# Retention and a bilinear feed-forward layer in one kernel: slots 8 to 11 as one tile, pairs of blocks by 7 products in both four-slot tiles, and a third order of the steps

## The chip, the cores and the metric

The kernel runs on one core of a Trainium2 chip. The time is microseconds of the device for one execution of the whole program, median of the runs; lower is better. The kernel before takes 218.17 us (median of 3 runs, 218.07 to 218.31).

The engines are named as in the profile: PE (TensorE, matrix products; PEld is its weight load), DVE (VectorE), ACT (ScalarE), POOL (GpSimd) and SP (SyncE, which only issues transfers here). Each engine works through its own list of instructions in the order in which the program emits them; engines wait for each other by semaphores.

## The reference

The input is q, k and v of shape 4 × 8 × 768 × 64 (batch, head, position, width) and the weights w_a, w_b (512 × 1536) and w_out (1536 × 512), all float32.

```python
    state = np.zeros((B, H, D, D), dtype=np.float32)
    y = np.zeros_like(q)
    for t in range(S):
        state = gamma[None, :, None, None] * state + np.einsum('bhd,bhe->bhde', k[:, :, t], v[:, :, t])
        y[:, :, t] = scale * np.einsum('bhd,bhde->bhe', q[:, :, t], state)
...
    x = np.ascontiguousarray(attn_out.transpose(0, 2, 1, 3)).reshape(B * S, H * D)
...
    a = x @ w_a
    b = x @ w_b
    return (a * b @ w_out).astype(np.float32)
```

The loop runs over the 768 positions, with gamma_h = 1 − 2^(−5−h) for head h and scale 1/8. The rest is one bilinear feed-forward layer over 3072 tokens.

## The kernel before, in words

**Slots and tiles.** The 3072 tokens are 24 slots of 128: slot t is chunk t mod 6 of batch t div 6. `TILES` (L16) groups the slots for the feed-forward layer: tiles of 4, 2, 2, 2, 2, 4 and 8 slots, so slots 8 and 9 are one tile, 10 and 11 the next, 12 to 15 the four-slot tile numbered 5, and 16 to 23 the last.

**Attention of one slot.** k and q are multiplied by tables of powers of gamma (`scaled`, L318: `kqb<-kf`, `kqb<-qf`, casts to bf16 on the way), v is cast (`vb`). SP turns k and q of a slot around with a transposing DMA (`flip`, L373, L376: `kqT<-kqb`). PE then makes the scores of keys and queries (`scores`, L407: `at<-kqT`; DVE masks them, `aT<-at,mask`, L421), adds k^T v to the state (`update`, L424: `st<-vb,kqb`; a cast to bf16, `gst<-st`), reads the earlier chunks through the state (`inter`, L446: `y<-kqT,gst`), adds the chunk's own part (`intra`, L457: `y<-aT,vb`), and ACT copies the result as columns of x (`leave`, L467: `xt<-y`). Scores of a slot need the turned k and q of both slots of its pair. `turn(new, old)` (L477) makes the scores and states of one pair of slots and the outputs of an earlier pair in one visit.

**The feed-forward layer of a tile.** For each of 12 blocks of 128 columns of the hidden layer, `ffn_a` (L611) and `ffn_g` (L625) make four matmuls each over the tile's tokens (512 columns for four slots, 256 for two). ACT casts the a side (`asb<-a`), and DVE multiplies it with the g side straight from PSUM (`ht<-g,asb`, L633).

**Seven products for eight.** Where two halves times two halves of a matrix product are wanted, the kernel uses a scheme with 7 products and sums ahead of and behind them. The output of each tile from the second on is made this way by class `Group` (products of six 256-column matmuls, `mA`, `mB`, `mC`; sums `hs` of the hidden layer by `hsum`; `wsum` of the weights; results `osb`). In the last tile, all of the hidden layer is made this way by class `Unit` (`uA`, `uB`, `uC`, with weight sums `wea`, `web`, `wsa`, `wsb` from `weight_piece` and `xs` from `x_sum`). In tile 5, `Quad` (L983 on) does so for two of six pairs of blocks (block p and p + 6, p = 0 and 1), a and b separately, each in half banks of 256 columns: ACT copies an intermediate result (`snapf<-fa`, 256 wide), DVE adds and multiplies in 256-wide pieces; `xf` are sums of x.

**What sets the order.** It is written out by hand, in functions that emit one step behind the other: `casts(t)` scales k, q and v of a slot on POOL, turns them on SP and issues the loads of slot t + 2; `blocks(J, a, b)` emits hidden blocks; `single(J, …)` laces a tile's output products with the next tile's first three blocks; `laced` (with the string `LACED`) does it for the tile with pairs; `big` (strings `START` and `END`) is the last tile. Output stores wait in a list until `store()` issues them from SP. PSUM has eight banks: three in a ring for blocks (`Ring`), two for y, two for at, one for st.

Of the kernel before, what the change touches and what calls it, by code (L numbers as in the profile page):

```python
# [9 lines left out]
F32 = mybir.dt.float32  # L10
# [5 lines left out]
TILES = [4, 2, 2, 2, 2, 4, 8]  # L16
# [3 lines left out]
START = ("A1 A2 u0.1 u1.1 A6 T X3 A7 B1 X2 A5 B6 B7 X1 A3 B5 u0.2 u1.2 B2 X4 A4 u0.6 B3 u1.6 B4 u0.5 u1.5 "  # L20
         "u0.7 u2.1 u0.3 u1.7 u2.6 u1.3 u0.4 u2.2 u3.1 u2.5 u1.4 u2.7 u3.6")
END = ("u11.1 u10.5 u10.7 u9.4 u11.6 u10.3 u11.2 S03 a1< u11.5 u11.7 u10.4 b1< u11.3 a1> b1> c1< d1< u11.4 a7 c1> d1> c2 d2 "
       "S02 S01 b7 a2 b2 S04 a6 b6 S13 a5 b5 S12 a3 b3 a4 b4 S11 c7 d7 c6 d6 S14 c5 d5 "
       "c3 c4 d4 d3")
V_LATE = range(12, 20)
LACED = ("X3 X2 m1 m7 m2 a1 b1 a2 b2 m6 X1 a6 b6 a7 b7 F2 X4 m5 a5 b5 K20 G2 a3 b3 a4 b4 V18 "
         "m3 c1 d1 F3 H3 c2 d2 c6 d6 c7 d7 c5 d5 m4 c3 d3 V19 c4 d4 G3")
# [4 lines left out]
def kernel(  # L32
# [78 lines left out]

    def raw_tile(shape, dtype, tag, name):
        return raw.tile(shape, dtype, tag=tag, name=name, bufs=3 if tag == "vf" else 2)
# [3 lines left out]
    def load_slot(t, names="kqv"):  # L117
        b, ci = divmod(t, NCH)
        for nm in names:
            src = {"k": k, "q": q, "v": v}[nm]  # L120
            if nm == "q":
                if t % 2 == 0:
                    load_two(nm, src, b, ci // 2, t)
                continue
            if t % 2 == 0:
                whole[nm] = raw_tile([P, 2, H, D], F32, nm + "f", nm + "f")
            raws[nm, t] = whole[nm][:, t % 2]
            s = src[b, :, ci * P : (ci + 1) * P, :].rearrange("h p d -> p h d")
            seq(nc.sync.dma_start(out=raws[nm, t], in_=s))

    def load_slots(t):
        for u, names in ((t, "kq"), (t + 1, "k"), (t, "v"), (t + 1, "v")):
            load_slot(u, names)

    def load_two(nm, src, b, u, t):
        f = raw_tile([P, H, 2, D], F32, nm + "f", nm + "f")
        s = src[b, :, 2 * u * P : 2 * (u + 1) * P, :].rearrange("h (p two) d -> p h two d", two=2)
        seq(nc.sync.dma_start(out=f, in_=s))  # L138
# [38 lines left out]
    def issue_loads(n):  # L177
        for _ in range(min(n, len(pending))):
# [4 lines left out]
            elif what[0] in "kqv":  # L183
                load_pair_q(n) if what[0] == "q" else load_two(what[0], {"k": k, "v": v}[what[0]], 0, n, 2 * n)
            else:
                {"p": load_pair, "s": load_slots, "t": load_slot, "w": load_w, "o": load_o}[what[0]](n)


    kqb = {}
# [113 lines left out]
    def cast_o(j):  # L303
        cast(nc.gpsimd, wo_bf[:, j * FPO : (j + 1) * FPO, :], wst["o", j])
# [12 lines left out]
    def scaled(eng, t, i):  # L317
        if i and t < 2 * PAIRS:  # L318
# [12 lines left out]
        else:  # L331
            dst = dst.rearrange("p hp r d -> p r hp d")
# [3 lines left out]

    def new_nat(t):
        kqb[t] = nat.tile([P, 2, HP, 2, D], BF16, tag="kqb", name="kqb")
        kb[t], qb[t] = kqb[t][:, 0], kqb[t][:, 1]
        vb[t] = nat.tile([P, H, D], BF16, tag="vb", name="vb")  # L340

    def casts(t, between=lambda: None):
        new_nat(t)
        scaled(nc.gpsimd, t, 0)
        between()
        scaled(nc.gpsimd, t, 1)
        if t not in range(12, 20):
            cast(nc.gpsimd, vb[t], raws["v", t])
        u = t + 2
        if u == 20:  # L350
            load_slot(u, "kq")
        flip(t)
        if u == 20:
            load_slot(u + 1, "k")
            return
        if u == 21:
            load_slot(u - 1, "v")
            load_slot(u, "v")
            load_slot(22, "kq")
            return  # L360
        if u in V_LATE:
            if u == 13:
                load_slot(12, "q")
            elif u == 19:
                load_slot(18, "kq")
            load_slot(u, {12: "k", 18: ""}.get(u, "kq"))
            if u % 2:
                load_slot(u - 1, "v")
                load_slot(u, "v")
        elif u < NSLOT:  # L370
            load_slot(u)

    def flip(t):  # L373
        if t % 2 == 0:
            kqT[t // 2] = tra.tile([P, 2, 2, HP, P], BF16, tag="kqT", name="kqT", bufs=3)
        seq(nc.sync.dma_start_transpose(  # L376
            out=kqT[t // 2][:, t % 2].rearrange("p a b c -> p (a b) c"),
            in_=kqb[t].rearrange("p a hp r d -> p (a hp r d)")))

    def late_kq(t):  # L380
        for u in (t, t + 1):
            new_nat(u)
            scaled(nc.gpsimd, u, 0)
            scaled(nc.gpsimd, u, 1)
            flip(u)
        if t == 20:
            load_slot(23, "k")
            load_slot(22, "v")
            load_slot(23, "v")

    def casts_two(t):
        for u in (t, t + 1):
            new_nat(u)
            scaled(nc.gpsimd, u, 0)
            scaled(nc.gpsimd, u, 1)
            flip(u)
        for u in (t, t + 1):
            cast(nc.gpsimd, vb[u], raws["v", u])
        load_slot(t + 3)
# [9 lines left out]
    def scores(t, where, cuts=2):  # L409
        at = score_banks(where)  # L410
# [13 lines left out]
    def update(t, eng):  # L424
        ci = t % NCH
        if ci == NCH - 1:
            return
# [17 lines left out]

    def inter(t):  # L446
        if t % NCH == 0:
            return
        for j in range(2):
# [8 lines left out]
    def intra(t):  # L458
        for r in range(2):
# [7 lines left out]
    def leave(t):  # L467
        J, i = where[t]
# [7 lines left out]

# [846 lines left out]
```

## Time and profile before

| what | value |
|---|---|
| median of the runs | 218.17 us (218.07 to 218.31, 3 runs) |
| the profiled execution | 218.26 us |
| its span on the core | 216.6 us |
| granted PE clock | 1.0 in every slice |
| busy: PE, DVE, ACT, POOL | 209.8, 151.1, 105.1, 155.5 us |
| instructions of PE, DVE, ACT, POOL | 2250, 277, 236, 187 |

The profile is one execution, taken by the hardware profiler. Its page gives busy time by engine, the span in 40 slices (each digit is tenths of busy time), the chain of work that ended last, and groups of instructions. A group's row reads: line, engine, operation, out<-in, partitions x elements, count | busy us, mean ns of one | idle time of the engine just before them and what ended it. A timeline row reads: start us, duration us (of a run of equal instructions), engine, line, operation, count. In a row of the view of waits stand the engine and what waited, what it waited for, and total us, times, longest. Matmuls overlap in PE's pipeline, so what one costs is read from the distance between starts and not from its duration.

### The profile page before, as it was taken

Reading aid. Unit: us, or ns where it says so; the run is one execution under the profiler, and the core shown is the slowest. Engines: PE = TensorE matmul, PEld = TensorE weight load, DVE = VectorE, ACT = ScalarE, POOL = GpSimd, SP = SyncE. Lnnn points to the kernel's source line nnn. Section 1 sums busy time; section 2 is a strip of 40 time slices with the busy share of each in tenths; the row PEclk is TensorE's granted clock in tenths of the full one; section 3 lists DMA queues with packets and bytes.
Section 4 is the critical chain, followed back from the end, with each engine's and each line's share of the span. In section 5 each row is a group of like instructions: output and inputs, shape, how many; then the busy total and the mean of one; then the engine's idle time right before and its main releaser. Section 6 shows DMA issues by size and latency. Waiting matters only on the chain.

```text
span 216.6 us, 5726 instructions
## 1 busy us (share of the span) xinstructions
PE 209.8 (97%) x2250; PEld 145.8 (67%) x2250; DVE 151.1 (70%) x277; ACT 105.1 (49%) x236; POOL 155.5 (72%) x187
## 2 busy tenths in 40 slices
PE   7789999999999999999999999999999999999994
PEld 3458445587458888888888877557864444458883
DVE  5796347845985486356377978686577887688952
ACT  3175325343224444464576475657545656652331
POOL 7277877778889487979959979799996999530000
PEclk9999999999999999999999999999999999999999
DMA  6999999999999999399989999980013000000055
GB/s 181 315 337 370 377 360 357 363 237 240 227 267 235 173 254 280 76 189 257 213 187 227 222 200 215 236 139 3 5 73 122 0 0 3 2 0 0 27 194 170
DMA packets 82906, 39.68 MB, mean 183 GB/s; under 512 B 57536, under 2 KB 75840, under 8 KB 82880
## 3 DMA queue, kind: packets, MB, share of 16 engines
q1 hardware_dynamic: 82736, 39.26, 74.4%
q8 instruction: 17, 0.28, 0.5%
q10 hardware_dynamic: 144, 0.07, 0.1%
q14 instruction: 9, 0.07, 0.1%
HBM read 28.31 MB, written 6.29 MB: 160 GB/s over the span
## 4 chain that ended last, share of the span: by engine, by line
PE 91%; SPq 3%; DMA 3%; POOL 0%; issue 0%; DVE 0%
PE a L619 18%; PE g L631 18%; PE mA L739 12%; PE uA L913 10%; PE mB L739 6%; PE o L656 5%; PE uB L913 5%; DMA wsta<-in_moe_w_a_dram 3%; PE mC L739 3%; PE at L415 2%; PE uC L913 2%; SPq L150 2%; PE y L463 2%; PE st L433 2%; PE fa L1003 2%; SPq L138 1%
## 5 line engine op out<-in xcount | busy, mean ns | idle before, releaser
L633 DVE TENSOR_TENSOR ht<-g,asb 128x256 bf16<-128x256 f32 (+1 forms) x70 | 34.4, 493 | 30.3 <-PE g L631 27.1
L619 PE MATMUL a<-xt,wa_bf 128*128 128x256 bf16 (+1 forms) x280 | 48.6, 300 | 0.2 <-POOL wa_bf L287 0.2
L631 PE MATMUL g<-xt,wb_bf 128*128 128x256 bf16 (+1 forms) x280 | 48.4, 300 | 0.0
L622 ACT CAST asb<-a 128x256 bf16<-128x256 f32 (+1 forms) x70 | 30.0, 428 | 33.5 <-PE a L619 31.3
L631 PEld LDWEIGHTS <-wb_bf 128*128 128x128 bf16 x280 | 27.1, 98 | 10.2
L619 PEld LDWEIGHTS <-wa_bf 128*128 128x128 bf16 x280 | 26.5, 98 | 10.8 <-POOL wa_bf L287 0.6
L920 ACT COPY snap<-uA 128x512 f32<-128x512 f32 x36 | 20.0, 587 | 15.4 <-PE uA L913 13.9
L335 POOL TENSOR_TENSOR kqb<-kf,ktab 128x512 bf16<-128x512 f32 x22 | 22.9, 1045 | 5.3 <-DMA kf<-in_k_dram 4.9
L739 PEld LDWEIGHTS <-hs 128*128 128x128 bf16 x234 | 22.8, 98 | 3.6
L421 DVE TENSOR_TENSOR aT<-at,mask 128x512 bf16<-128x512 f32 x36 | 22.3, 683 | 0.3
L335 POOL TENSOR_TENSOR kqb<-qf,qtab 128x512 bf16<-128x512 f32 x18 | 19.8, 1100 | 2.6 <-DMA qf<-in_q_dram 1.6
L672 POOL TENSOR_TENSOR ht<-gsb,asb 128x512 bf16<-128x512 bf16 x13 | 15.2, 1174 | 7.5 <-DVE gsb L672 7.4
L746 ACT COPY snaps<-mA 128x256 f32<-128x256 f32 x30 | 11.0, 374 | 18.9 <-PE mA L739 18.9
L672 POOL TENSOR_TENSOR hs<-ht 128x384 bf16<-128x384 bf16 (+3 forms) x14 | 15.8, 1130 | 5.7 <-DMA kf<-in_k_dram 3.2
L739 PEld LDWEIGHTS <-ht 128*128 128x128 bf16 x180 | 17.5, 98 | 3.3
L672 POOL TENSOR_TENSOR hs<-ht,hs 128x384 bf16<-128x384 bf16 (+1 forms) x17 | 16.8, 993 | 2.5 <-DVE ht L633 2.3
L739 PE MATMUL mA<-wsum,hs 128*128 128x256 bf16 x120 | 15.2, 273 | 0.0
L672 DVE TENSOR_TENSOR osb<-mB,snaps 128x256 f32<-128x256 f32 x20 | 8.4, 422 | 8.2 <-ACT snaps L746 4.3
L287 POOL CAST vb<-vf 128x512 bf16<-128x512 f32 x12 | 7.8, 668 | 5.2 <-DMA vf<-in_v_dram 5.2
L656 PE MATMUL o<-wo_bf,ht 128*128 128x512 bf16 x48 | 10.7, 379 | 0.0
L672 DVE TENSOR_TENSOR gsb<-uB,snap 128x512 bf16<-128x512 f32 x12 | 8.2, 686 | 2.9 <-ACT snap L920 2.1
L672 DVE TENSOR_TENSOR asb<-uB,snap 128x512 bf16<-128x512 f32 x12 | 8.2, 685 | 2.9 <-ACT snap L920 2.0
(148 smaller groups left out, 379.8 us busy)
## 6 DMA issues: line engine op xcount, KB each, us to landing
out_dram<-osb SPq DMA_DIRECT2D x21, 256.0 KB, 3.9
kf<-in_k_dram SPq DMA_DIRECT2D x18, 256.0 KB, 4.9
qf<-in_q_dram SPq DMA_DIRECT2D x9, 512.0 KB, 5.8
vf<-in_v_dram SPq DMA_DIRECT2D x18, 256.0 KB, 5.1
wsta<-in_moe_w_a_dram SPq DMA_DIRECT2D x6, 512.0 KB, 7.2
wsto<-in_moe_w_out_dram SPq DMA_DIRECT2D x6, 512.0 KB, 8.7
wstb<-in_moe_w_b_dram SPq DMA_DIRECT2D x5, 512.0 KB, 7.9
kf<-in_k_dram SPq DMA_DIRECT2D x3, 512.0 KB, 7.4
```

What stands on the lines that cost most here:

```text
L335: seq(eng.tensor_tensor(dst, src, tab, op=ALU.mult))
L421: seq(nc.vector.tensor_tensor(aT[t][:, r], at[r], mask.to_broadcast([P, HP, P]), op=ALU.mult))
L619: seq(nc.tensor.matmul(a, wa_bf[:, kt, fs], xcols(J, kt, c0, c1), start=(kt == 0), stop=(kt == KT - 1)))
L622: seq(nc.scalar.copy(asb, a))
L631: seq(nc.tensor.matmul(g, wb_bf[:, kt, fs], xcols(J, kt, c0, c1), start=(kt == 0), stop=(kt == KT - 1)))
L633: seq(nc.vector.tensor_tensor(ht[J][:, ft, c0:c1], g, asbs.pop((J, ft, c0)), op=ALU.mult))
L656: seq(nc.tensor.matmul(o, ht[J][:, ft, i * P : (i + 1) * P], wo_bf[:, ft], start=(ft == 0), stop=(ft == NFT - 1), skip_group_check=True))
L672: seq(eng.tensor_tensor(dst, x, y, op=op))
L739: seq(nc.tensor.matmul(m, w, right[:, j], start=(first and j == 0), stop=(j == NP - 1), skip_group_check=True))
L746: seq(nc.scalar.copy(self.snaps[:, n], self.bank["A"]))
L913: seq(nc.tensor.matmul(m, w, right[:, k], start=(first and k == 0), stop=(k == 1), skip_group_check=True))
L920: seq(nc.scalar.copy(self.snaps[n], self.bank["A"]))
```

## The change

- `TILES` becomes [4, 2, 2, 4, 4, 8]: slots 8 to 11 are one tile (number 3), 12 to 15 the next (number 4). Hidden blocks of slots 8 to 11 are made with 512 columns.
- Class `Duo` takes the place of `Quad`, and both four-slot tiles make two of six pairs of blocks with 7 products for 8. a and b stand side by side in one bank of 512 columns: one ACT copy of 512 (`snapf<-fA`), one DVE sum of 512 (`ab<-fC,snapf`), then a product of the two halves of `ab` (256 wide, on DVE or POOL). The matmuls stay 256 wide.
- From the second tile's first block on, every step stands in a table, `ORDER`, that a loop at the end carries out. A letter is the kind of step (a and g hidden blocks, M a step of a group, d of a pair by 7 products, u of a unit; k, y and v the scaling and casts of a slot; f its transposing DMA; l a load; U, S, I, N, L state, scores, inter, intra and leave; h, W, w, x, X sums; C a weight cast; s the stores), then come its numbers, and at the end the engine (D DVE, G POOL, A ACT) or queue (S SP, A ACT). Everything up to the last block of the first tile is emitted as before.
- k or q of a slot can be scaled on ACT, then as eight instructions of 128x64, one per head. This is done for k of slots 6, 8 and 18 and q of slots 7, 9 and 10. k of slot 11 and 17, and q of 15 and 17, go to DVE (of the later slots, q of 21 and k of 22 too). Two loads are issued on ACT's queue.

The diff, cut to what the text below speaks of:

```diff
-TILES = [4, 2, 2, 2, 2, 4, 8]
+TILES = [4, 2, 2, 4, 4, 8]
...
+DUO = {3: {0: ('F', 'b', 'F', 'DGG', 'KKT'), 1: ('F', 'Z', 'F', 'DGG', 'OTO')}, 4: {0: ('F', 'b', 'F', 'DGG', 'KKT'), 1: ('F', 'Z', 'F', 'DGG', 'OTO')}}
...
+ORDER = """
...
+h.3.3.4.6.D s k.17.D g.3.11 g.3.10 h.3.4.0.4.D k.18.A s y.18.G f.17.S h.3.2.4.6.G h.3.4.4.6.D M.3.0.7
+l.q.20.S M.3.0.1 I.15 I.14 v.16.G h.3.1.4.6.D f.18.S N.14 l.v.19.S l.q.22.S U.15.D N.15 l.k.20.S M.3.0.2
...
@@ scaled @@
+            if eng is nc.scalar:
+                for h in range(H):
+                    seq(nc.scalar.mul(dst[:, h % HP, h // HP, :], src[:, h, :], tab[:, h, :]))
+                return
...
+    class Duo:
...
         def leave(self, i, c, bank, n):
-            cols = slice(c * DH, (c + 1) * DH)
-            if self.w == "a":
-                tt(self.half(i)[:, cols], self.bank[bank], self.snaps[n], ALU.add)
-                return
-            h = ht[5][:, NP * i + self.p, cols]
-            tt(h, self.bank[bank], self.snaps[n], ALU.add)
-            tt(h, h, self.half(i)[:, cols], ALU.mult, nc.vector if (i, self.p) == (0, 0) else nc.gpsimd)
+            ab = asbp.tile([P, 4 * P], BF16, tag="asb", name="ab")
+            tt(ab, self.bank[bank], self.snaps[n], ALU.add)
+            ft = NP * i + self.p
+            done.add(("h", self.J, ft, c))
+            tt(ht[self.J][:, ft, c * DH : (c + 1) * DH], ab[:, :DH], ab[:, DH:], ALU.mult, self.engines["CBA".index(bank)
+               if bank == "C" else 1 + int(n == 1)])
...
+    for step in ORDER.split():
+        kind, *args = step.split(".")
+        STEPS[kind](*args)
```

How the steps move on the engines is shown at two places.

**Slots 6 and 7.** Before, POOL's list behind the casts of w_out and ahead of the first scores (kqb_1046 is slot 6, kqb_1052 slot 7, kqb_1101 slot 8):

```order
L287 CAST wo_bf_190<-wsto_559 128x1024
L335 TENSOR_TENSOR kqb_1046<-kf_561,ktab1_376 128x2x4x64
L335 TENSOR_TENSOR kqb_1046<-qf_563,qtab_378 128x2x4x64
L335 TENSOR_TENSOR kqb_1052<-kf_561,ktab1_376 128x2x4x64
L335 TENSOR_TENSOR kqb_1052<-qf_563,qtab_378 128x2x4x64
L287 CAST vb_1047<-vf_566 128x512
```

Now, ACT's list at the end of the second tile's hidden blocks (asb are its a blocks, kqb_1028 is slot 6, kqb_953 slot 7, kqb_1069 slot 8):

```order
L348 CAST wo_bf_190<-wsto_551 128x1024
L650 CAST asb_1020<-a_1015 128x256
L401 ACTIVATE kqb_1028<-kf_561,ktab1_376 128x64 x8
L650 CAST asb_1057<-a_1052 128x256
L401 ACTIVATE kqb_953<-qf_563,qtab_378 128x64 x8
L401 ACTIVATE kqb_1069<-kf_569,ktab1_376 128x64 x8
L348 COPY osb_1109<-o_1088 128x512
```

k of slot 6 and q of slot 7 have moved from POOL to ACT, among the casts of the a blocks; the other two (k of slot 7, q of slot 6) stay on POOL. The transposing DMAs of both slots on SP stand behind these.

**Slots 16 and 17.** Before, POOL scaled both (kqb_2304 is slot 16, kqb_2445 slot 17; hs are sums of the tile of slots 10 and 11):

```order
L335 TENSOR_TENSOR kqb_2304<-kf_2112,ktab1_376 128x2x4x64
L335 TENSOR_TENSOR kqb_2304<-qf_2114,qtab_378 128x2x4x64
L672 TENSOR_TENSOR hs2_2298<-ht_2037,hs3_2252 128x3x128
L672 TENSOR_TENSOR hs1_2300<-ht_2037 128x3x128
L672 TENSOR_TENSOR hs4_2302<-ht_2037,hs2_2298 128x3x128
L335 TENSOR_TENSOR kqb_2445<-kf_2112,ktab1_376 128x2x4x64
L335 TENSOR_TENSOR kqb_2445<-qf_2114,qtab_378 128x2x4x64
```

Now, DVE's list from the scores of slot 15 to those of slot 17 (ht_1746 is the hidden layer of slots 8 to 11, g_2149 its block g(3,5), kqb_1966 slot 17, aT_2308 the masked scores of slot 17):

```order
L454 TENSOR_TENSOR aT_2129<-at1_2112,mask_179 128x512
L662 TENSOR_TENSOR ht_1746<-g_2149,asb_2147 128x512
L699 TENSOR_TENSOR hs3_1999<-ht_1746 128x512
L406 TENSOR_TENSOR kqb_1966<-kf_1844,ktab1_376 128x2x4x64
L662 TENSOR_TENSOR ht_1746<-g_2164,asb_2160 128x512
L662 TENSOR_TENSOR ht_1746<-g_2170,asb_1997 128x512
L699 TENSOR_TENSOR hs4_2176<-ht_1746,hs2_2107 128x1024
L699 TENSOR_TENSOR hs4_2176<-ht_1746,hs2_2107 128x512
L699 TENSOR_TENSOR hs1_2066<-ht_1746 128x512
L350 CAST gst0_180<-st_1935 128x256
L699 TENSOR_TENSOR osb_2269<-mC_2262,snaps_2207 128x256
L454 TENSOR_TENSOR aT_2308<-at0_2290,mask_179 128x512
```

k of slot 17 has moved from POOL to DVE, between a sum of the hidden layer of slots 8 to 11 and the products of its last two blocks. SP's list now (kqT_2061 takes slots 16 and 17, kqT_2230 slots 18 and 19):

```order
L191 DMA vf_2109<-in_v_dram 128x8x64
L191 DMA kf_2070<-in_k_dram 128x8x64
L428 DMA_TRANSPOSE kqT_2061<-kqb_1966 128x8x128
L201 DMA qf_2198<-in_q_dram 128x8x128
L428 DMA_TRANSPOSE kqT_2230<-kqb_2178 128x8x128
L191 DMA vf_2109<-in_v_dram 128x8x64
```

Slot 17's transposing DMA stands on SP behind the loads of slots 18 and 19 and ahead of the loads of slots 20 to 23; the transposing DMA of slot 16 went out before those loads.

More of the change, by code (lines that the diff above doesn't have):

```diff
@@ L467, in leave @@
     def leave(t):
+        need(*((x, u) for x in "NI" for u in (t, t + 1)))
+        done.update((("x", t), ("x", t + 1)))
         J, i = where[t]
@@ L612, in ffn_a @@
         c1 = TILES[J] * P if c1 is None else c1
+        if J > 1:
+            need(*(("x", t) for t in range(sum(TILES[:J]), sum(TILES[: J + 1]))))
         if J not in ht:
@@ L626, in ffn_g @@
         c1 = TILES[J] * P if c1 is None else c1
+        done.update(("h", J, ft, c) for c in range(2))
         fs = slice(ft * P, (ft + 1) * P)
@@ L959, in p3 @@
             else:
+                done.update(("h", (BIG, 1), self.p, x) for x in range(2))
                 tt(h_big(1)[:, self.p], self.bank["A"], half_a.pop(key), ALU.mult)
@@ L1290, with group, duo @@
[L1290 to L1292 removed]
+    done.update(("h", J, ft, c) for J in (0,) for ft in range(NFT) for c in range(2))
+    done.update(("U", t) for t in range(6))
+    engine = {"D": nc.vector, "G": nc.gpsimd, "A": nc.scalar}
+    made = {}
+    def group(J, i):
+        if (J, i) not in made:
+            made[J, i] = Group(J, i, *GROUPS[J, i])
+        return made[J, i]
+    def duo(J, p):
+        if (J, p, "duo") not in made:
+            made[J, p, "duo"] = Duo(J, p, *DUO[J][p])
+        return made[J, p, "duo"]
```

617 lines of the change are left out of this document (254 added, 363 removed).

## The prediction

> **What bounds the kernel now.** I read the page first: the busy shares, the 40 slices and the chain that ended last.
>
> ```profile
> span 216.6 us, 5726 instructions
> PE 209.8 (97%) x2250; PEld 145.8 (67%) x2250; DVE 151.1 (70%) x277; ACT 105.1 (49%) x236; POOL 155.5 (72%) x187
> PE   7789999999999999999999999999999999999994
> PEclk9999999999999999999999999999999999999999
> PE 91%; SPq 3%; DMA 3%; POOL 0%; issue 0%; DVE 0%
> ```
>
> PE is busy 97% of the span at the full granted clock, every slice from the fourth to the last but one is full, and the chain is 91% PE. What PE waits for, by the view of waits:
>
> ```profile
> PE idle L603 <- DVE zero L193: 1.5, 1, 1.5
> PE tp L524 <- DVE kqb L323: 0.7, 2, 0.5
> PE tp L524 <- DVE kqb L335: 0.6, 1, 0.6
> PE at L538 <- ACT xt L285: 0.5, 1, 0.5
> PE a L619 <- POOL wa_bf L287: 0.2, 1, 0.2
> ```
>
> All five (lines L524 to L619) are of the start, which the change leaves alone. So the time behind the start is the sum of PE's work, and the change can win only by a shorter sum and lose only by waits that PE does not have now. A busy PE still hides small gaps; the timeline shows them as starts that lie too far apart:
>
> ```profile
> 99.05 0.60 PE L619 MATMUL a<-xt,wa_bf 128*128 128x256 bf16 x4
> 99.56 0.60 PE L631 MATMUL g<-xt,wb_bf 128*128 128x256 bf16 x4
> 112.42 0.60 PE L619 MATMUL a<-xt,wa_bf 128*128 128x256 bf16 x4
> 112.94 0.60 PE L631 MATMUL g<-xt,wb_bf 128*128 128x256 bf16 x4
> 113.49 0.60 PE L619 MATMUL a<-xt,wa_bf 128*128 128x256 bf16 x4
> 42.98 0.60 PE L619 MATMUL a<-xt,wa_bf 128*128 128x256 bf16 x4
> 43.41 0.60 PE L631 MATMUL g<-xt,wb_bf 128*128 128x256 bf16 x4
> ```
>
> A block of four takes 0.43 to 0.44 us from start to start (42.98 to 43.41), but 0.51, 0.52 and 0.55 at the other three: 0.07 to 0.11 us lost at each, 0.27 in all. That is all there is to win from gaps.
>
> **Term 1, PE's products.** The start to start of a wide block:
>
> ```profile
> 22.39 1.03 PE L631 MATMUL g<-xt,wb_bf 128*128 128x512 bf16 x4
> 23.26 1.03 PE L619 MATMUL a<-xt,wa_bf 128*128 128x512 bf16 x4
> ```
>
> Four matmuls of 512 columns take 0.864 us (216 ns each; the rows give 0.87), four of 256 take 0.4365 (109.2 each; mean of neighbouring starts). Counted along PE's rows in the order, matmuls of blocks and of pairs by 7 products with 256 columns go from 472 to 336, those with 512 from 144 to 208. So −136 × 109.2 ns + 64 × 216 ns = −14.85 + 13.82 = **−1.03 us**. The saving is real columns (2048 fewer) plus the small fixed part of 72 matmuls. It lies on PE and therefore on the path.
>
> **Term 2, changes of the array's shape.** Attention's matmuls use pieces of the array. The trace names the shape of each group:
>
> ```profile
> 115.67 0.60 PE L631 MATMUL g<-xt,wb_bf 128*128 128x256 bf16 x4
> 116.20 0.73 PE L415 MATMUL at<-kqT 64*64 64x128 bf16 x32
> 116.72 0.44 PE L453 MATMUL y<-kqT,gst 64*64 64x128 bf16 x16
> 117.08 0.32 PE L433 MATMUL st<-vb,kqb 128*64 128x64 bf16 x8
> 117.23 0.62 PE L463 MATMUL y<-aT,vb 128*64 128x128 bf16 x16
> 117.78 0.61 PE L619 MATMUL a<-xt,wa_bf 128*128 128x256 bf16 x4
> ```
>
> From 115.67 to 116.20 there are 0.53 us for a block that takes 0.437 between its like: 0.093 us for the step into another shape. The third order cuts attention into more visits: scores, state and outputs stand alone more often. Along the rows, PE changes shape 66 times instead of 59. Seven more at 0.093 are **+0.65 us**; bounds are 0 and 0.65, since a change could lie under a weight load, but no such step in the rows is free.
>
> **Term 3, the scores of slot 17.** Before, POOL scales k and q of slots 16 and 17, SP turns them (transposing DMAs), and PE needs them far later:
>
> ```profile
> 105.90 3.38 SPq L376 DMA_TRANSPOSE kqT<-kqb  x2
> DMA to landing us min/median/max: 3.0/4.5/6.0
> ```
>
> The second has left SP at 109.28, and the scores start at 116.20. Now k of slot 17 is scaled on DVE behind g(3,5) and an hs sum, and only then may SP issue the transpose. The prices:
>
> ```profile
> L633 DVE TENSOR_TENSOR ht<-g,asb 128x512 bf16<-128x512 f32 x18 | 12.3, 690 | 10.0 <-PE g L631 9.8
> L672 DVE TENSOR_TENSOR hs<-ht 128x512 bf16<-128x512 bf16 x1 | 1.0, 1043 | 0.0
> L672 DVE TENSOR_TENSOR hs<-ht,hs 128x512 bf16<-128x512 bf16 x1 | 0.8, 821 | 0.1
> L335 DVE TENSOR_TENSOR kqb<-kf,ktab 128x512 bf16<-128x512 f32 x2 | 1.3, 688 | 0.6 <-DMA kf<-in_k_dram 0.6
> L287 DVE CAST gst<-st 128x256 bf16<-128x256 f32 x1 | 0.4, 425 | 0.7 <-PE st L433 0.7
> 196.00 0.43 DVE L672 TENSOR_TENSOR ht<-gsb,asb 128x512 bf16<-128x512 bf16 x1
> 117.35 1.88 DVE L421 TENSOR_TENSOR aT<-at,mask 128x512 bf16<-128x512 f32 x3
> ```
>
> Back to back, a 512-wide instruction with its source in PSUM takes 0.63 us (1.88 for three), some 0.06 less than its duration. Counted from the end of g(3,5): 0.2 handoff (an estimate: the timeline's usual distance from PE to its reader) + 0.63 (ht) + 0.8 (hs, between 0.43 and 1.04) + 0.69 (k) = 2.3 us; then issue to landing 3.0, 4.5 or 6.0: landed at 5.3, **6.8** or 8.3. PE needs it after three wide blocks (2.59), four group products of six 256-column matmuls (4 × 0.655 = 2.62) and one visit of attention (y twice 16, st 8, by the rows above 0.36 + 0.09 + 0.15 + 0.55 = 1.15): 6.4 us. Stall: 0 at the short landing, 0.4 at the median, 1.9 at the long one (2.2 if hs also costs 1.04). I take **+0.4**. SP's later loads and the flips behind this one wait as well, but nothing of them is due within 5 us.
>
> **Term 4, DVE where the two four-slot tiles meet.** Behind the same g(3,5) stand ten DVE rows: three ht of 512, k, hs of 512, hs4 of 1024 and of 512, hs1 of 512, the state's cast gst. In pitches 3 × 0.63 + 0.63 + 3 × 0.8 + 0.95 + 0.36 = 6.2 us (nine rows, the tenth an osb of 0.36 behind the cast). PE's next state update overwrites the bank that gst reads, 7.4 us after g(3,5) (6.4 above and 1.0 of scores). A margin of 1.0 remains, and it is gone when the four SBUF-only sums cost 1.04 for 0.8. In the stretch before it, DVE has the six 512-wide sums of the two pairs by 7 products, the xf sums, and the scores of slots 12 to 15, which come earlier than before; I work its load out to about 0.9 of PE's time by the durations above. Before, DVE was busy 13.66 us of 22 between 100 and 122 us:
>
> ```profile
> 100.00:122.00 22.00, 22.00 (x315) 19.11 (x313) 13.66 (x28) 12.07 (x31) 18.86 (x22) 1.00 1.03 217
> ```
>
> At that 0.62 PE already lost 0.27 us in the gaps above. Four more such handoffs at 0.1 give **+0.4**; the bounds are 0 (all fit) and 1.4 (six SBUF-only sums, each 0.24 dearer, on the path).
>
> What makes them dear is seen in the rows: 0.43 us at 196.00, where POOL has nothing, and 1.04 where it works. The Trainium skill, "SBUF — State Buffer", section "Who interferes with whom", says that a DVE instruction with two SBUF inputs contends with a GpSimd instruction that reads SBUF, and that the loser waits for the whole of the other. The trace agrees so far (0.43 against 1.04). By that rule the upper bound of term 4 holds wherever POOL is busy, which is the second rival below.
>
> **Term 5, slots 6 and 7 on ACT.** k of slot 6 and q of slot 7 leave POOL and become eight 128x64 activations each, one per head:
>
> ```profile
> L217 ACT ACTIVATE ktab<-earg 128x48 f32<-128x48 f32 x2 | 0.5, 254 | 0.0
> L268 ACT ACTIVATE qtab<-earg,bq 128x48 f32<-128x48 f32 x1 | 0.3, 343 | 0.0
> L622 ACT CAST asb<-a 128x256 bf16<-128x256 f32 x52 | 19.4, 374 | 20.2 <-PE a L619 18.7 <-DVE osb L672 0.7
> 52.59 7.93 PE L656 MATMUL o<-wo_bf,ht 128*128 128x512 bf16 x36
> 60.69 0.64 PE L415 MATMUL at<-kqT 64*64 64x128 bf16 x32
> ```
>
> The shape itself is not in the trace; 254 ns (no operand beside the input) and 343 (with one per partition, as here) bound it. ACT can start five blocks before the outputs begin at 52.59: 52.59 − 5 × 0.437 + 0.2 + 0.37 = 51.0. With 16 × 0.30 + 0.37 the last is done at 56.2 (55.4 or 56.9 by the bounds), landed at 60.7 by the median, just as PE asks at 60.69. Bounds 0 and 2.2 (0.343 and a landing of 6.0); I take **+0.1**. The Trainium skill, "VectorE: DVE Perf Modes", section "The TRN2 errata — SBUF-src ops pay a fixed extra latency per instruction", gives 224 cycles plus the elements at 1.2 GHz for such a ScalarE operation, by estimate 0.24 us; the sum by it would have no wait here. No row here shows that shape.
>
> **At nothing.** Moved v casts, wo casts, weight pieces and two loads on ACT's queue: POOL (72%) and ACT (49%) have room, and PE's rows need their results later by microseconds; if that cover fails, one late weight piece costs its own 0.7 us. Slots 22 and 23, late before, are scaled earlier now. The tail keeps its last instructions, so the 1.66 us around the span (218.26 − 216.6) and the final store stay.
>
> **Sum.** −1.03 + 0.65 + 0.4 + 0.4 + 0.1 = +0.52 us on the profiled 218.26, that is 218.78. That execution is 0.09 above the median of 218.17, so I forecast **218.7**.
>
> **The rivals.**
> - *Not slower: every handoff fits.* If the transpose of slot 17 lands in under 4.1 us from its issue and DVE's SBUF sums cost at most 0.8, terms 3 to 5 vanish: 218.17 − 0.38 = 217.8, and 217.5 if the old gaps go as well. For it: the three short bounds all allow it. Against it: three chains must all fall on the good side. Chance 0.2.
> - *Contention with POOL* (the page's rule above): term 4 at 1.4, and hs on slot 17's chain at 1.04 (term 3 at 0.6): 218.17 − 0.38 + 2.0 + 0.1 = 219.9. It decides once the SBUF sums pass 1.0. Chance 0.15.
> - *Slot 17 lands late*: term 3 at 1.9 to 2.2, the others as taken: 220.3. It decides once issue to landing passes 5.5 us; the longest seen is 6.0. Chance 0.13.
> - *Slots 6 and 7 late*: activations at 0.343 and a long landing, term 5 at 2.2: 220.8. Chance 0.07.
> - *The products cost as much as the blocks they replace*: that would need matmuls of 256 columns dearer than 109 ns inside the pairs; then term 1 shrinks toward 0: 219.7. Nothing in the rows speaks for it. Chance 0.03.
>
> The forecast itself (218.2 to 219.2) has 0.42. A measurement here tells about 0.2% (0.44 us) from no change. Below 217.73 lies most of the first rival, 0.15. Between 217.73 and 218.61 lie the rest of it and some two fifths of the forecast's case, 0.25. Above lies 0.6. The range that leaves out 2 in 10 is 217.7 to 220.4.
>
> **What would show it.** Term 1: the counts of 256- and 512-column matmuls and unchanged pitches. Term 2: steps of 0.09 at each new visit. Term 3: PE waiting for the DMA of kqT ahead of the scores of slots 17 and 16 near 115 us. Term 4: waits of PE on DVE (aT, gst, osb) from 100 to 120 us, and SBUF sums near 1 us. Term 5: the activations' mean and a wait at the first scores near 60.7 us. I am wrong if PE shows none of these waits, or one at a place I have not named.

## The result, and the profile after

| | median | ratio to the kernel before (95% interval) |
|---|---|---|
| before | 218.17 us (218.02 to 218.78, 5 runs) | |
| after | 219.87 us (219.51 to 220.33, 5 runs) | 1.0074 (1.0054 to 1.0094) |

The changed kernel is slower by 0.74%, some 1.6 us; the forecast was 218.7. Ratios leave disturbed executions out, so they need not be the quotient of the medians. The profiled execution took 219.51 us (before 218.26), with a span of 217.8 (before 216.6). It is the fastest of the five, which matters below.

The page after, the same parts as before:

```profile
span 217.8 us, 5526 instructions
PE 208.7 (96%) x2161; PEld 138.4 (64%) x2178; DVE 162.6 (75%) x288; ACT 113.8 (52%) x264; POOL 134.3 (62%) x154
PE   7889999999999999999997999999999999999993
PEclk9999999999999999999999999999999999999999
PE 87%; DMA 3%; DVE 3%; SPq 3%; issue 1%; POOL 0%; ACT 0%; ACTq 0%; DVEq 0%
```

PE is busy 1.1 us less and the span is 1.2 longer. The row of PE now has a 7 in the 22nd slice (114 to 120 us), and DVE has got into the chain (3%). The view of waits names the place:

```profile
PE st L470 <- DVE gst L350: 1.1, 1, 1.1
PE fA L1010 <- DVE xf L699: 0.3, 1, 0.3
```

Both are new (the other waits in that view are of the start): the state update of slot 16 waits for a cast on DVE, and a pair's product waits for a sum of x (`xf`). PE's timeline at the first:

```profile
114.15 0.82 PE L761 MATMUL mA<-wsum,hs 128*128 128x256 bf16 x6
114.89 0.64 PE L448 MATMUL at<-kqT 64*64 64x128 bf16 x32
116.63 0.32 PE L470 MATMUL st<-vb,kqb 128*64 128x64 bf16 x8 [1.09 <-DVE gst L350]
```

The scores of slots 17 and 16 started on time at 114.89; it is the update behind them that stood. DVE's timeline up to the cast, POOL's at the same time, and the SP row of the load that POOL asked for:

```profile
109.44 0.43 DVE L699 TENSOR_TENSOR hs<-ht 128x512 bf16<-128x512 bf16 x1
109.78 0.68 DVE L406 TENSOR_TENSOR kqb<-kf,ktab 128x512 bf16<-128x512 f32 x1
110.44 1.49 DVE L662 TENSOR_TENSOR ht<-g,asb 128x512 bf16<-128x512 f32 x2
111.84 1.37 DVE L699 TENSOR_TENSOR hs<-ht,hs 128x1024 bf16<-128x1024 bf16 x1
114.26 0.80 DVE L699 TENSOR_TENSOR hs<-ht,hs 128x512 bf16<-128x512 bf16 x1 [1.04 <-POOL hs L699]
114.98 1.26 DVE L699 TENSOR_TENSOR hs<-ht 128x512 bf16<-128x512 bf16 x1
116.17 0.41 DVE L350 CAST gst<-st 128x256 bf16<-128x256 f32 x1
```

```profile
111.63 1.04 POOL L406 TENSOR_TENSOR kqb<-qf,qtab 128x512 bf16<-128x512 f32 x1 [2.55 <-DMA qf<-in_q_dram]
112.63 1.60 POOL L699 TENSOR_TENSOR hs<-ht,hs 128x512 bf16<-128x512 bf16 x1
```

```profile
105.06 1.38 SPq L201 DMA_DIRECT2D qf<-in_q_dram  x1
```

Read from the bottom: the load of q of slots 18 and 19 leaves SP at 106.4, and POOL has it at 111.6. POOL stands 2.55 us for it, scales q (1.04), and only then makes the sum hs2 (1.60). DVE stands 1.04 us for hs2, then needs 0.80 and 1.26 for its two sums, and casts the state at 116.17. PE stood for that from 115.5 on.

Three things lie on this chain, and the load is the smallest of them. hs2 adds up the last two blocks of the tile (10 and 11), whose products DVE ends at 111.93 (the row at 110.44), so POOL could not have begun it before. It began at 112.63, so the load made it at most 0.7 us late. The handoff itself, from DVE to POOL and back, is the 1.04 us. And the two sums behind it are dear: in this trace, DVE's sums of 128x512 bf16 with both inputs in SBUF take 0.41 to 0.43 us in all ten places where POOL has no instruction (109.44 is one), and up to 1.26 where it has. At 0.42 each, the cast would have come some 1.2 us earlier, by estimate, which is the whole wait of PE.

Where the 1.25 us of the two profiled executions lie: up to the second tile's first block the after run is 0.49 shorter (that block starts at 41.50 instead of 41.99; the same instructions, and in the profiles of the other versions it starts between 41.73 and 42.74, so chance). From there to the last group of matmuls it needs 172.27 us instead of 170.94, +1.33. Behind that, up to the span's end, 4.03 instead of 3.67, +0.36 (the last stores land later). Outside the span 0.05. The sum is −0.49 + 1.33 + 0.36 + 0.05 = +1.25. And the +1.33 are −1.03 (products) + 0.49 (shapes, below) + 1.16 (the wait for gst) + 0.49 (the wait for the xf sum; both by the distance of the starts) + about 0.2 of small gaps.

### The profile page after: what moved, and what is told of

The parts are those of the page before. It is cut to its first block, busy times and chain, and to the rows that moved or that the text cites. A ratio compares the mean times of both kernels' runs of the same rounds, so it can differ in the third digit from the quotient of the medians.

```text
span 217.8 us, 5526 instructions
## 1 busy us (share of the span) xinstructions
PE 208.7 (96%) x2161; PEld 138.4 (64%) x2178; DVE 162.6 (75%) x288; ACT 113.8 (52%) x264; POOL 134.3 (62%) x154
## 4 chain that ended last, share of the span: by engine, by line
PE 87%; DMA 3%; DVE 3%; SPq 3%; issue 1%; POOL 0%; ACT 0%; ACTq 0%; DVEq 0%
PE a L647 16%; PE g L660 16%; PE mA L761 12%; PE uA L911 9%; PE mB L761 6%; PE o L683 5%; PE uB L911 5%; DMA wsta<-in_moe_w_a_dram 3%; PE mC L761 3%; PE fA L1010 3%; PE y L510 2%; PE uC L911 2%; PE at L448 2%; SPq L213 2%; PE st L470 1%; PE fB L1010 1%
## 5 line engine op out<-in xcount | busy, mean ns | idle before, releaser
L662 DVE TENSOR_TENSOR ht<-g,asb 128x256 bf16<-128x256 f32 (+1 forms) x54 | 29.1, 550 | 19.5 <-PE g L660 16.9
L647 PE MATMUL a<-xt,wa_bf 128*128 128x256 bf16 (+1 forms) x209 | 40.5, 322 | 0.6 <-POOL wa_bf L350 0.2
L660 PE MATMUL g<-xt,wb_bf 128*128 128x256 bf16 (+1 forms) x214 | 40.0, 323 | 0.1
L660 PEld LDWEIGHTS <-wb_bf 128*128 128x128 bf16 x216 | 20.8, 98 | 12.9 <-issue 0.2
L647 PEld LDWEIGHTS <-wa_bf 128*128 128x128 bf16 x216 | 20.1, 98 | 11.8 <-POOL wa_bf L350 0.5
L406 POOL TENSOR_TENSOR kqb<-kf,ktab 128x512 bf16<-128x512 f32 x16 | 17.5, 1102 | 9.9 <-PE at L448 5.8
L406 POOL TENSOR_TENSOR kqb<-qf,qtab 128x512 bf16<-128x512 f32 x12 | 14.0, 1168 | 10.2 <-DMA qf<-in_q_dram 6.7
L699 POOL TENSOR_TENSOR hs<-ht,hs 128x512 bf16<-128x512 bf16 (+2 forms) x10 | 12.3, 1237 | 7.8 <-DVE ht L662 5.2
L699 POOL TENSOR_TENSOR hs<-ht 128x768 bf16<-128x768 bf16 (+4 forms) x11 | 14.0, 1273 | 3.8 <-DVE ht L662 3.7
L523 ACT CAST xt<-y 128x512 bf16<-128x512 f32 x18 | 9.7, 591 | 5.2 <-PE y L510 2.9
```

The lines of the kernel that those rows point to most:

```text
L406: seq(eng.tensor_tensor(dst, src, tab, op=ALU.mult))
L647: seq(nc.tensor.matmul(a, wa_bf[:, kt, fs], xcols(J, kt, c0, c1), start=(kt == 0), stop=(kt == KT - 1)))
L660: seq(nc.tensor.matmul(g, wb_bf[:, kt, fs], xcols(J, kt, c0, c1), start=(kt == 0), stop=(kt == KT - 1)))
L662: seq(nc.vector.tensor_tensor(ht[J][:, ft, c0:c1], g, asbs.pop((J, ft, c0)), op=ALU.mult))
L699: seq(eng.tensor_tensor(dst, x, y, op=op))
```

## The experiments

All ratios are to the kernel before on the same chip. The table of steps is the only thing edited, except in e11, which edits the kernel before.

| run | median, us | ratio (95% interval) |
|---|---|---|
| e1_gst_act | 220.20 | 1.0092 (1.0062 to 1.0122) |
| e2_hs2_dve | 219.85 | 1.0106 (1.0040 to 1.0173) |
| e3_q18_first | 219.58 | 1.0062 (1.0038 to 1.0087) |
| e4_no_pairs3 | 221.86 | 1.0174 (1.0157 to 1.0190) |
| e5_k22_pool | 218.86 | 1.0037 (1.0019 to 1.0054) |
| e6_hs2_k22 | 219.34 | 1.0045 (1.0017 to 1.0073) |
| e7_all_waits | 218.46 | 1.0011 (0.9982 to 1.0040) |
| e8_more_shapes | 219.32 | 1.0054 (1.0027 to 1.0080) |
| e9_keep_hs2 | 218.79 | 1.0020 (0.9994 to 1.0046) |
| e10_one_visit | 218.70 | 1.0029 (1.0007 to 1.0051) |
| e11_before_k23_dve | 225.76 | 1.0364 (1.0342 to 1.0386) |
| e12_loads_on_pool | 218.66 | 1.0037 (1.0013 to 1.0061) |

**The cast on another engine.**

```diff
-U.15.D
+U.15.A
```

> The changed kernel, with the state's cast behind slot 15 (gst) on ACT in place of DVE, nothing else. In the profile of the changed kernel PE waits 1.09 us for it ahead of the state update of slot 16 at 116.6 us. Theory A (the wait is only this cast's place, behind two sums hs4 and hs1 in DVE's list): the wait goes, about 1.1 us less, near 218.8 us, ratio to before 1.003. Rival B (DVE is overloaded there, and the next instruction of DVE that PE needs is as late): the wait comes back within 5 us at another PE row on DVE, gain under 0.3 us.

The wait for gst was gone from the profile and the time was not better. In that execution, the slowest of its six, PE waits four times for DVE, 0.3 to 0.5 us each. Two of these lie ahead of the cast that was moved (ht at 50.10 us, xf at 87.08), so they are not of this edit. The other two lie behind it: 0.54 us for the masked scores aT at 118.92, 1.8 us behind the state update, and 0.26 for ab at 133.92. So half of the wait came back at the next result of DVE that PE needs, and DVE stood 2.4 us for POOL's sums as a whole. Theory A fell by the median: moving the cast alone does not bring the 1.1 us.

**More work on DVE, one wait less.**

```diff
-h.3.2.4.6.G
+h.3.2.4.6.D
```

> The changed kernel, with the second sum hs2 (blocks 4 and 5) of slots 8 to 11 on DVE in place of POOL. Theory A (DVE stood idle 1.04 us in its list for that sum, which stood on POOL behind the scaling of q of slot 18, which waited for its load): though DVE gets 0.4 to 0.8 us more work, it does not wait, the cast gst comes about 1 us earlier, and PE's wait of 1.09 falls to under 0.4: 218.9 to 219.2 us. Rival B (DVE's load is the cause): the added work makes PE's wait 0.4 to 0.8 us longer, 220.3 to 220.7 us.

The wait ahead of the state update went away though DVE had more to do there, and so did the one for xf. That speaks against load as the cause of the first. But the time stayed, and in the profile a place came up that nobody had named. DVE, then PE:

```profile
131.00 1.15 DVE L406 TENSOR_TENSOR kqb<-kf,ktab 128x512 bf16<-128x512 f32 x1 [3.20 <-DMA kf<-in_k_dram]
132.07 0.68 DVE L699 TENSOR_TENSOR ab<-fB,snapf 128x512 bf16<-128x512 f32 x1
```

```profile
132.80 0.38 PE L1010 MATMUL fB<-xf,wa_bf 128*128 128x256 bf16 x2 [1.95 <-DVE ab L699]
```

k of slot 22 stands in DVE's list ahead of a pair's sum. PE arrived 1.7 us earlier than in the changed kernel, but the load came 1.2 us later (DVE starts on it at 131.00, in the changed kernel at 129.83). SP's row of that load (with the one of slot 23), in the changed kernel and in e2:

```profile
126.12 1.21 SPq L191 DMA_DIRECT2D kf<-in_k_dram  x2
```

```profile
127.28 1.21 SPq L191 DMA_DIRECT2D kf<-in_k_dram  x2
```

In both it stands on SP right behind the transposing DMA of slot 19, and DVE has it 3.7 us after SP begins to issue it. So when it comes is set by SP's list. What PE had won, DVE lost waiting for a transfer, and PE with it.

**The load of q earlier.**

```diff
-f.16.S s l.v.17.S h.3.1.0.4.G v.15.A l.k.18.S N.13 L.12
-U.13.A a.3.4 l.q.18.S g.3.4
+f.16.S s l.q.18.S l.v.17.S h.3.1.0.4.G v.15.A N.13 L.12
+U.13.A a.3.4 l.k.18.S g.3.4
```

> The changed kernel, with the load of q of slots 18 and 19 issued on SP ahead of the loads of v of slot 17 and k of slot 18 (it stood behind four others). If the first cause is this load (POOL was idle 2.55 us for it, up to 111.6 us), it lands some 2 us earlier, POOL's sum hs2 ends before DVE asks for it, and PE's wait of 1.09 us falls to 0.1 or less: 218.8 us. If the order of DVE's list alone is the cause, the wait stays over 0.8 us and the time at 219.6 to 219.9 us. If the other loads now come late, a new wait of k of slot 18 shows.

PE's wait for gst fell from 1.1 to 0.7 us, a part of what was expected; the ratio is not to be told from the changed kernel's. (In e5 below, whose edit lies behind this place, the same wait is 0.4, so a fall of this size can also be chance.) The rest is the handoff. DVE, then POOL:

```profile
111.59 1.27 DVE L662 TENSOR_TENSOR ht<-g,asb 128x512 bf16<-128x512 f32 x2
114.51 0.80 DVE L699 TENSOR_TENSOR hs<-ht,hs 128x512 bf16<-128x512 bf16 x1 [1.05 <-POOL hs L699]
```

```profile
109.74 1.04 POOL L406 TENSOR_TENSOR kqb<-qf,qtab 128x512 bf16<-128x512 f32 x1
112.94 1.53 POOL L699 TENSOR_TENSOR hs<-ht,hs 128x512 bf16<-128x512 bf16 x1 [2.16 <-DMA kf<-in_k_dram]
```

POOL scales q without a wait, and then stands until DVE's products are done at 112.86, since hs2 reads them. (The profile names a DMA for that wait; the sum begins 0.08 us behind the products, and in e10 the profile names them at the same row.) DVE again stands 1.05 us for hs2. It stands 1.04 or 1.05 us there in all seven profiles in which hs2 is on POOL, whether the load was late or not.

**Without pairs in the first four-slot tile.** On top of e1, the steps d.3 and x.3 are left out, and blocks 0, 1, 6 and 7 of the tile are made like the others:

```diff
-d.3.0.1
+a.3.0
...
-x.3.3.D
```

> As e1_gst_act, and in the tile of slots 8 to 11 the two pairs of blocks are made by 8 products as plain blocks (four more blocks a and g of 512 columns, no xf sums, no snapf copies) in about the same places. Term 1 of the prediction: 56 matmuls of 256 columns (6.12 us) give way to 32 of 512 (6.91 us): 0.80 us more than e1_gst_act. Rival (the pairs' 256-column products cost on PE what the blocks cost, or DVE's load eats the gain): within 0.2 us of e1_gst_act.

The median is 1.7 us over e1, more than expected, with waits of its own (1.0 on ab, behind k of slot 22). Between two rows with no wait between them the trace is clear. After, then e4, the outputs of slots 8 and 9 and the state update of slot 12:

```profile
81.41 0.42 PE L497 MATMUL y<-kqT,gst 64*64 64x128 bf16 x16
...
98.75 0.32 PE L470 MATMUL st<-vb,kqb 128*64 128x64 bf16 x8
```

```profile
81.72 0.42 PE L497 MATMUL y<-kqT,gst 64*64 64x128 bf16 x16
...
99.86 0.32 PE L470 MATMUL st<-vb,kqb 128*64 128x64 bf16 x8
```

17.34 us with pairs and 18.14 without: 0.80 us, the value of term 1 for one tile.

**k of slot 22 off DVE.**

```diff
-k.22.D
...
-v.21.A k.23.G
+v.21.A k.22.G k.23.G
```

> The changed kernel, with k of slot 22 scaled on POOL, just ahead of k of slot 23, in place of DVE. Theory C: what DVE and POOL scale in their lists waits for input loads that the transfers deliver at about the same time whatever PE does (k of slot 22 at 129.8 to 132.4 us in five profiles), and what stands behind it on DVE (ab of a pair) holds PE. In the changed kernel's own profile DVE waited 0.30 us for it and PE 0.1, in others up to 3.2 and 2.0. So here: no wait of DVE for a load near 130 us, PE's wait of about 1.1 ahead of the state update of slot 16 stays, and the time is 0.2 to 0.5 us shorter than the changed kernel's 219.87, that is 219.4 to 219.7. Rival B (DVE's load, not this wait): 0.7 us less work on DVE, the gain is spread and under 0.2.

This one step brings the ratio from 1.0074 to 1.0037, some 0.8 us, more than the 0.2 to 0.5 expected. In the changed kernel's profile, the fastest of its five executions, DVE waits 0.3 us for this load and PE loses nothing at the place:

```profile
130.43 0.82 PE L761 MATMUL mB<-wsum,ht 128*128 128x256 bf16 x6
132.38 0.38 PE L1010 MATMUL fB<-xf,wa_bf 128*128 128x256 bf16 x2
```

These 1.95 us are also the distance (1.95 or 1.96) in all seven profiles in which k of slot 22 is on POOL (e5 to e10 and e12). In the other four with it on DVE, the distance is 2.38 (e1), 4.07 (e2), 2.42 (e3) and 3.11 (e4). Over the five that is 0.8 us more in the mean, as much as the step brought in the medians. The wait depends on when the load comes, and one execution shows one draw of it. The expectation that PE's wait of 1.1 us for gst would stay was a miss: it is 0.41 here, though the edit lies behind it. That wait varies, too.

**Both, and then all named waits.** e6 is e2 and e5 together. e7 has in addition U.15.A, the load of q earlier, and x.4.1.D right behind x.4.2.D.

> e2_hs2_dve and e5_k22_pool together: hs2 (blocks 4 and 5) of slots 8 to 11 on DVE, k of slot 22 on POOL. In e2 the first change took PE's wait of 1.1 us at the state update away and the second place took 1.95 back. Theory C: both go, 218.0 to 218.3 us, ratio to before 0.999 to 1.001. Rival B (DVE overloaded from 100 to 125 us): waits of aT, osb or ab of 0.5 to 1 us stay there, 218.8 us or more.

> e6_hs2_k22, and gst behind slot 15 on ACT, the load of q of slots 18 and 19 ahead of v of 17 and k of 18, and the xf sum 1 of the second four-slot tile right behind sum 2. If all that the change loses are these waits, PE runs densely from 43 us on, and terms 1 and 2 of the prediction alone are left: 218.17 - 0.38 = 217.8 us (217.6 to 218.1), ratio 0.998. Rival (a new wait at the next thin place): 218.2 or more.

In the profile of e6 PE is dense from 42 us to the end (group of windows; columns are the stretch, its length, then busy us and counts of PE, PEld, DVE, ACT, POOL, clock, DMA share, GB/s). After first, then e6:

```profile
100.00:122.00 22.00, 20.75 (x262) 13.57 (x264) 18.61 (x31) 10.89 (x27) 12.25 (x11) 1.00 1.05 217
122.00:150.00 28.00, 27.31 (x361) 17.67 (x364) 22.93 (x39) 16.54 (x35) 19.39 (x21) 1.00 0.85 151
```

```profile
100.00:122.00 22.00, 22.00 (x275) 14.57 (x274) 19.57 (x35) 11.40 (x29) 11.22 (x9) 1.00 1.08 213
122.00:150.00 28.00, 28.00 (x366) 17.97 (x365) 21.65 (x38) 17.01 (x37) 20.59 (x23) 1.00 0.85 157
```

DVE is busy 19.57 of 22 us there and PE loses nothing: a DVE at 0.89 does not hold PE up if it need not wait itself. That execution took 218.43, from its second tile to the last matmuls 170.68 us against 170.94 before. But the twelve runs of e6 go from 218.21 to 220.45 with a median of 219.34; so most executions lose time that this one does not, and where they lose it no trace shows. e7 has the best median of the family and its ratio, 1.0011, cannot be told from 1 (nor can e9's below); the expected 217.8 was missed.

**More steps into another shape.**

```diff
-I.11 I.10 s l.q.16.S N.11
-h.2.4.0.3.D N.10
+I.11 N.11 s l.q.16.S I.10
+h.2.4.0.3.D N.10
```

and the same for slots 12 and 13, 14 and 15, 22 and 23.

> e7_all_waits, with inter and intra of four pairs of slots in turn (for one slot after the other), so that PE changes the array's shape eight times more; the same matmuls otherwise. Term 2 of the prediction: 8 x 0.093 = 0.74 us more than e7. Rival (a change of shape costs nothing of its own, and the steps seen at attention's borders come from something else): within 0.2 us of e7.

The medians differ by 0.86 us, but the intervals of the ratios overlap. The trace decides: one such visit after and in e8.

```profile
81.75 0.64 PE L510 MATMUL y<-aT,vb 128*64 128x128 bf16 x16
82.33 0.61 PE L647 MATMUL a<-xt,wa_bf 128*128 128x256 bf16 x4
```

```profile
81.75 0.31 PE L497 MATMUL y<-kqT,gst 64*64 64x128 bf16 x8
81.98 0.41 PE L510 MATMUL y<-aT,vb 128*64 128x128 bf16 x8
82.33 0.31 PE L497 MATMUL y<-kqT,gst 64*64 64x128 bf16 x8
82.56 0.41 PE L510 MATMUL y<-aT,vb 128*64 128x128 bf16 x8
82.91 0.61 PE L647 MATMUL a<-xt,wa_bf 128*128 128x256 bf16 x4
```

The same 32 matmuls take 0.92 us in two groups (81.41 to 82.33) and 1.16 in four: 0.12 for each step more. The other three visits of e8, against e7, give 0.24 to 0.25 too, 0.98 in all for eight.

**Back to POOL's sum, one visit less, every late load on POOL.** e9 is e7 with h.3.2.4.6.G again. e10 is e9 with U.6.A moved beside S.6. e12 is e7 with k.17.G behind k.16.G, f.17.S behind f.16.S, and k.18.G behind y.18.G.

> e7_all_waits, but with the sum hs2 (blocks 4 and 5) of slots 8 to 11 back on POOL, as in the changed kernel. So against the changed kernel: k of slot 22 on POOL, gst behind slot 15 on ACT, the load of q of slots 18 and 19 earlier, xf sum 1 earlier. Theory C (waits for loads inside DVE's list cost the time): 218.0 to 218.4 us, as e7. If DVE's wait for POOL's sum still matters, more than 218.8 us with PE waits near 117 us.

> e9_keep_hs2, and the state update of slot 6 beside the scores of slots 6 and 7, one visit in place of two. Term 2: one visit less, in the profile 0.15 to 0.25 us less between 57 and 63 us; the median 0.1 to 0.3 us under e9. Rival: the steps into another shape do not matter, within 0.05 us in the profile.

> e7_all_waits, and in addition k of slot 17 on POOL right behind k of slot 16 (it was on DVE), its transposing DMA issued right behind slot 16's, and k of slot 18 on POOL behind its q (it was on ACT, which in e9's profile stood 3.15 us for that load while PE stood 1.25 behind it). So no instruction of DVE or ACT between 100 and 135 us waits for a load that can be late; POOL takes these waits. Theory C: PE dense in nearly every execution, 217.8 to 218.2 us, and runs within 0.5 us of each other like the kernel before. Rival (the tight order itself, DVE at 0.85 of PE's time, makes the spread): the median stays at 218.4 or more with runs up to 220 us.

e9's profile shows an execution of 220.84 us, and in it a late transposing DMA of slot 17, which the changed kernel's profile did not show. ACT, then PE:

```profile
113.89 2.02 ACT L401 ACTIVATE kqb<-kf,ktab 128x64 bf16<-128x64 f32 x8 [3.15 <-DMA kf<-in_k_dram]
```

```profile
116.21 0.81 PE L761 MATMUL mA<-wsum,hs 128*128 128x256 bf16 x6 [1.25 <-ACT snaps L768]
118.42 0.64 PE L448 MATMUL at<-kqT 64*64 64x128 bf16 x32 [1.40 <-DMA kqT<-kqb]
```

ACT stood for the load of k of slot 18 with a copy behind it that PE needed, and slot 17's transposing DMA, which had left SP between 112.38 and 114.64, was late for the scores. k of slot 17 was ready at 111.13, and SP was still issuing two loads. The load of k of slot 18 left SP from 107.05 on, in the changed kernel from 103.67 on: in e9, as in e3, the load of q goes ahead of it. So both waits come at least in part from SP's list. e10, with the same order there, has neither in its profile. There the visit saves about 0.11 us by the starts, under the 0.15 to 0.25 expected, and the medians (218.70 against 218.79) are too close to tell. In e12's profile no instruction of ACT waits for a load and DVE only at the start and in sum 0.7 us, as the edit meant; ten of its twelve runs lie between 218.10 and 219.74. The median of 218.66 is the rival's: with the named waits gone, 0.4 us and most of the spread stay. Where that one execution loses its time can be read from the distances of PE's starts: 0.40 us at 49.69 (a g block that waits for ht), 0.30 in the visit at 103.56 (1.45 us instead of 1.15), 0.24 at 117.35 and 0.16 at 119.48, behind a sum hs1 that takes 1.26 us on DVE with POOL at work. The profile names a load for none of the four. With them the stretch from the second tile to the last matmuls is 171.30 us against 170.94 before; without them it would be 170.2, by estimate.

**The mechanism in the other kernel.** The kernel before, with one step of `late_kq` changed:

```diff
-            scaled(nc.gpsimd, u, 0)
+            scaled(nc.vector if u == 23 else nc.gpsimd, u, 0)
```

> The kernel before, with k of slot 23 scaled on DVE in place of POOL, nothing else. In its profile POOL got that load at 138.7 us and stood idle 1.11 us for it, which nobody felt. DVE reaches this instruction at about 133.5 us, with the masks of the scores of slots 18 and 19 behind it. Theory C (a load's wait inside DVE's list stops PE): PE stops until about 139.5, 2.5 to 5 us more, 220.5 to 223 us. Rival B (only DVE's load counts): 0.7 us more on an engine at 70%, 218.0 to 218.5 us.

DVE, then PE, then the windows behind it:

```profile
133.05 0.69 DVE L633 TENSOR_TENSOR ht<-g,asb 128x512 bf16<-128x512 f32 x1
138.95 1.33 DVE L335 TENSOR_TENSOR kqb<-kf,ktab 128x512 bf16<-128x512 f32 x1 [5.21 <-DMA kf<-in_k_dram]
```

```profile
140.94 1.86 PE L631 MATMUL g<-xt,wb_bf 128*128 128x512 bf16 x4 [5.22 <-DVE aT L421]
```

```profile
141.00:143.00 2.00, 2.00 (x5) 0.65 (x5) 1.77 (x4) 0.00 (x0) 0.29 (x1) 0.50 1.08 199
143.00:146.00 3.00, 3.00 (x13) 1.27 (x12) 1.23 (x3) 1.10 (x2) 0.00 (x0) 0.81 0.29 100
```

One instruction of 0.7 us, moved from POOL to DVE, costs 7.7 us. The load comes at 138.95, as on POOL before (138.7); DVE stands 5.21 us and PE 5.22. That is more than forecast. The wait alone is 5.22, and the granted clock is 0.50 in the two microseconds behind it and 0.81 in the next three, which by estimate costs 1.6 more (2 × 0.50 + 3 × 0.19); the profiled execution is 7.0 us longer than that of the kernel before.

## Why the prediction was right in its direction, and wrong in a size

The time is above the forecast's own case and on the second rival's 219.9, but not by that rival's sum: PE waited for gst and for an xf sum, nothing was lost at slot 17, and a wait that no term had (k of slot 22) came in. That the misses of terms 2 to 5 partly cancel is luck.

- **Term 1 (−1.03)** held where it was tested: 0.80 us for the two pairs of the tile between two rows of after and e4, as worked out. The other 0.23, wide blocks for narrow ones in slots 8 to 11, no run tests by itself; wide blocks still start 0.86 to 0.87 us apart in the changed kernel.
- **Term 2 (+0.65)** came out a little smaller. The visits of attention sum to 15.40 us before (11 visits) and 16.68 − 1.16 = 15.52 after (15 visits, without the wait); four more entries at 0.093 make +0.49. The seven more changes of shape were counted rightly, and in e8 a change inside a visit costs 0.12.
- **Term 3 (+0.4)** is 0 in the profiled execution (SP issued the transposing DMA from 110.50 on, right behind the scaling of k, and the scores started at 114.89 without a wait). In that of e9 the scores wait 1.4 us for it, but there SP's other loads held it, not the chain on DVE that the term adds up. So a late slot 17 can hold PE; that k on DVE makes it late is not shown.
- **Term 4 (+0.4) was the step that failed, by its size.** The place and the instructions were right: the cast gst, behind hs4 and hs1 in DVE's list, ahead of the state update of slot 16. It cost 1.16 us, and the xf sum, a place that the prediction had not named, 0.49 more. I had added up what DVE does (6.2 us against 7.4) and left out what it waits for. From g(3,5)'s product to the end of the cast DVE took 7.9 us (108.72 to 116.58): 1.04 of the 1.6 more are the wait for POOL's hs2, and the sums cost only some 0.3 more than the 0.8 and 0.95 that I had put in, since one was cheap (0.43) and the others were dear (0.80, 1.26, and 1.37 for 1024 columns). That is the mechanism of the second rival, but the term already held 0.8 us for each such sum of 512, so little was left of it. The rule of the Trainium skill ("SBUF — State Buffer", section "Who interferes with whom"), that a DVE instruction with two SBUF inputs contends with a GpSimd instruction that reads SBUF, fits the trace: 0.41 to 0.43 us in ten places with POOL idle, 0.42 to 1.26 in the 17 with POOL at work. In the kernel with hs2 on DVE (e2) the last of the sums took 0.42, and so did the xf sum that PE had waited for (1.26 in the changed kernel). That e2 took both the handoff and dear sums away at once leaves open how much of PE's wait each is worth.
- **Term 5 (+0.1)** was 0. The row of the shape that was missing before (here k of slot 8, right behind q of slot 7), SP's row of slot 7's transposing DMA, and the scores:

```profile
54.70 2.01 ACT L401 ACTIVATE kqb<-kf,ktab 128x64 bf16<-128x64 f32 x8
54.83 1.88 SPq L428 DMA_TRANSPOSE kqT<-kqb  x1
60.53 0.64 PE L448 MATMUL at<-kqT 64*64 64x128 bf16 x32
```

  These activations start 0.239 us apart; the row's 2.01 us holds the last one's whole 0.34. That agrees with the Trainium skill's 0.24 ("VectorE: DVE Perf Modes", section "The TRN2 errata — SBUF-src ops pay a fixed extra latency per instruction"). The prediction had bounded the distance of starts by two durations (0.254 and 0.343), and both were too long. The last of the sixteen ended at 54.80 instead of 56.2; the transposing DMA of slot 7 left SP by 56.71, and the scores at 60.53 did not wait.
- **"At nothing" was wrong in one point**: the scalings moved to DVE and ACT were priced by their length. k of slot 22 on DVE (e5) is worth some 0.8 us of the 1.6, because it waits for its load in a list that PE depends on.

So the change has a gain of about 0.5 us on PE (−1.03 + 0.49), and it loses that and 1.6 us more at places where PE waits for DVE. Two of them carry most of it: k of slot 22, a wait for a load, shown by e5 and by the twelve profiles, and with the same mechanism in the other kernel by e11; and the cast gst, a handoff to POOL and dear sums, shown by the rows of after, e2 and e3. e7, which takes away all waits named before it, comes to 1.0011 (0.9982 to 1.0040). What stays open is the rest: why e10 and e12 still stand 0.3 to 0.4% over the kernel before (e7 and e9 cannot be told from it), with executions of 220 us and more. In e12's profile it is four short waits and gaps, 1.1 us in sum; each of the others is known by one execution, too. No version tried is shown to beat the kernel before.

## What to carry to other kernels

A step that waits for a transfer belongs in the list of an engine that nobody is waiting for; here a scaling of 0.7 us cost 0.8 us in one kernel and 7.7 in the other. When work is moved between engines, list for each moved instruction what it waits for and what stands behind it, and add those waits to the sum, not only the durations. That holds for transfers and for sums that another engine makes: a sum sent to POOL and needed back on DVE cost DVE 1.04 us each time. To move a load earlier, look at what stands ahead of it in the issuing engine's list. And where the time hangs on when loads land, one profile is one draw: several executions, or the spread of the runs, show whether an order has room.

## What was not expected of the hardware

After PE's idle stretch of 5.22 us in e11 the granted clock was 0.50 between 141 and 143 us and 0.81 between 143 and 146. A wait of 1.95 us (e2) left it at 1.00.

DVE or POOL began on a load 3.7 to 4.1 us after SP had begun to issue it, where they stood waiting: for k of slot 22 in after, e1, e2 and e3 and for k of slot 23 in the kernel before and e11. SP began for slot 22 at 126.12 (after), 126.67 (e3), 127.28 (e2) and 128.38 us (e1), for slot 23 at 134.74 and 134.86. That the transfers come at about the same time whatever PE does, as the expectation of e5 has it, is not shown: the times follow SP's list, and before and e11 differ only behind that load.

DVE's sums of 128x512 bf16 from SBUF had two prices in one trace, 0.41 to 0.43 us with POOL idle and up to 1.26 with POOL at work.
